# Layer norm's scaling on VectorE, with mean and power as its two scalars

## The chip, the cores and the metric

The kernel runs on one core of a Trainium2 chip. The metric is the device time of one execution in microseconds (us), as the median of several runs. Beside it stands one execution that the hardware profiler recorded.

## What is computed

All of it is float32, for 8 batches of 576 tokens and 512 channels. Three blocks follow one another: an attention without a score matrix, a gated MLP with a mixing over tokens, and a spatial product of rank 32 with a channel MLP. The change lies in the second block:

```python
h = x @ w_in
h = 0.5 * h * (1.0 + np.tanh(c * (h + 0.044715 * h ** 3)))
u, v = (h[..., :d_ff // 2], h[..., d_ff // 2:])
mu = np.mean(v, axis=-1, keepdims=True)
var = np.mean((v - mu) ** 2, axis=-1, keepdims=True)
v_n = (v - mu) / np.sqrt(var + 1e-06) * g_ln
v_s = np.einsum('ts,bsd->btd', w_sg, v_n) + b_sg[None, :, None]
gated = u * v_s
x = x + gated @ w_out
```

The layer norm goes over the 512 columns of v, for each token.

## The kernel before, in words

There are two stages. In the first, until about 600 us, the kernel goes through the batches 0 to 7; in the second it does the large channel products for all tokens, in five groups. Beside the first stage the weights of the channel products are converted and written back to memory (tiles stg, f, chw), a piece at a time, on ScalarE, GpSimd and VectorE. Every product is made of float32 pieces: an operand is split into a high part (a ScalarE copy) and a low part (a subtraction, `low`, on VectorE or GpSimd), and three products are summed.

A batch b goes as follows. x comes as xh and xl. Then, for the five tiles t of 128 tokens (the fifth has 64), `emit_Vh` multiplies x by half of w_in into a PSUM tile pv, and ScalarE's gelu writes it to the SBUF tile ge (three buffers; L616, L620). `stats` takes mean and variance into the two columns of mv (L626 to L628), on VectorE: bn_stats, bn_aggr and the addition of epsilon; GpSimd then raises the second column to the power -0.5 (L629). `emit_ln` (L632) scales: VectorE makes shift = -mean * power (the tile sh, L636), ScalarE does ge = ge * power + shift (L639), ScalarE copies ge to the high part vh, and the low part vl is subtracted by GpSimd, for the fifth tile by VectorE, into the upper half of vh. All five vh and vl stay until the mixing over tokens, `emit_S` (PSUM tile pS, L671).

The loop at L1284 calls `emit_ln` for tile t - 1 behind `stats` of tile t, and for the fifth tile behind the first product of `emit_Uh` (PSUM tiles pu, L657; there are four, and gelu takes them to ut). Between the tiles stand other pieces of work: the transposed y of the batch before (yh, yl), its rank-32 product (pp, pst) and the addition of its result to y (`emit_PV`, PSUM tile pw, VectorE's addition yt, L762), and for the next batch the maxima of q (qm) and of k (km; `k_max` transposes the folded maximum, PSUM tile pm, L423). pv, pw, pu, pS and py share three PSUM buffers ("big"). After `emit_Uh` come the exponentials of the next batch's q and k, `emit_S`, and `emit_y` with the product by w_out (py), whose operands gh and gl are the split gated tile gt.

What sets the order: TensorE's and, in the batch loop, VectorE's instructions run in the order in which the program names them (`manual_schedule`, `in_order(dve)`). The queues of ScalarE, GpSimd and SP, which issues the DMAs, are ordered in the batch loop when the program is built, by a simulated timeline. In the second stage all are in program order.

In batch 7 the buffers of ge are reused for the tiles us, with which the second stage's operands uh and ul are made (`u_parts`, L794; the load is L800).

Of the kernel before, what the change touches and what calls it, by code (L numbers as in the profile page):

```python
# [8 lines left out]
F32 = mybir.dt.float32  # L9
F32R = mybir.dt.float32r  # L10
U32 = mybir.dt.uint32
AF = mybir.ActivationFunctionType
ALU = mybir.AluOpType
# [9 lines left out]
def fused_kernel(tc, q, k, v, w_in, g_ln, w_sgT, b_sg, w_out, U, V, w_ch1, w_ch2, outT):  # L23
    nc = tc.nc
    B, S, C = q.shape
    P = 128
# [22 lines left out]
    pe, act, dve, pool, sp = nc.tensor, nc.scalar, nc.vector, nc.gpsimd, nc.sync  # L49
# [10 lines left out]
    def copy(out, src):  # L60
        return act.activation(out, src, AF.Copy)  # L61

    def low(eng, out, src, hi):
        return tt(eng, out, src, as_f32(hi), ALU.subtract)

    def opened(name, bufs=1, **kw):
        cm = tc.tile_pool(name=name, bufs=bufs, reuse_waits="tile", **kw)
        return cm.__enter__(), lambda: cm.__exit__(None, None, None)
# [17 lines left out]
    tmpp, close_tmpp = opened("tmpp", 2, side="left")  # L86
# [545 lines left out]
    def emit_ln(b, t):  # L632
        ge, mv = ln.pop((b, t))
        n = TR[t]
        shift = tmpp.tile([P, 1], F32, tag="sh", name="sh", bufs=4)
        dve.scalar_tensor_tensor(  # L636
            out=shift[0:n], in0=mv[0:n, 0:1], scalar=-1.0, in1=mv[0:n, 1:2], op0=ALU.mult, op1=ALU.mult
        )
        act.activation(ge[0:n], ge[0:n], AF.Identity, bias=shift[0:n], scale=mv[0:n, 1:2])  # L639
        h = wrk.tile([P, F], F32R, tag=f"vh{t}", name=f"vh{t}")  # L640
        if t < NT:
            l = wrk.tile([P, F], F32R, tag=f"vl{t}", name=f"vl{t}")
            copy(h, ge)
            low(pool, l, ge, h)
            vh[b, t] = (h, l)
        else:
            copy(h[0:R], ge[0:R])
            low(dve, h[64 : 64 + R], ge[0:R], h[0:R])
            vh[b, t] = h
# [620 lines left out]
    for b in range(B):  # L1270
# [13 lines left out]
        for t in range(NT + 1):  # L1284
            emit_Vh(b, t)
            if nxt:
                with behind(dve):
                    for t2 in Q_MAX[b > 0][t]:
                        q_max(nxt, t2)
                    for _ in range(FOLDS[b > 0][t]):  # L1290
                        next(fold)
            if t < NT:
                stats(b, t)
            slot(TURNS[b][0][t])
            if t > 0:
                emit_ln(b, t - 1)
            if t == NT:
                stats(b, t)
            if b > 0:
                for t2 in ((2,), (3, 4), (), (), ())[t]:  # L1300
                    emit_yT(b - 1, t2)
            if t == 2 and b > 0:
                for t2 in range(NT + 1):
                    emit_U(b - 1, t2)
            if b > 0:
                for c in ((), (), (), (0, 1), (2, 3))[t]:
                    emit_PV(b - 1, c)
# [16 lines left out]
        for f in range(NF):  # L1324
            if nxt and f == spread_at:
                k_spread(nxt)
            if b == 0:
                slot(TURNS[b][1][f])
            if not nxt:
                for _ in range((0, 2, 2, 2)[f]):  # L1330
                    next(prep, None)
            emit_Uh(b, f)
            if f == 0:
                emit_ln(b, NT)
                if nxt:
                    load_v(nxt)
                else:
                    next(prep, None)
            if nxt:
                for t in Q_SUB[b > 0][f]:  # L1340
                    q_sub(nxt, t, pool if t in Q_SUB_POOL[b > 0] else dve)
                for t in K_SUB[b > 0][f]:
                    if f >= spread_at:
                        k_sub(nxt, t)
                    else:
                        late_k.append(t)
                if f == spread_at:
                    for t in late_k:
                        k_sub(nxt, t)
            if b > 0:  # L1350
                slot(TURNS[b][1][f])
# [181 lines left out]
```

## Time and profile before

| | us |
|---|---|
| median of 3 runs | 1314.13 |
| lowest and highest run | 1310.84 and 1314.26 |
| the profiled execution | 1313.29 |
| its span, from the first to the last instruction | 1311.5 |

| engine | busy us | share of the span | instructions |
|---|---|---|---|
| TensorE (PE) | 1261.5 | 96% | 7576 |
| VectorE (DVE) | 982.4 | 75% | 1426 |
| ScalarE (ACT) | 654.9 | 50% | 997 |
| GpSimd (POOL) | 346.2 | 26% | 440 |

The mean granted TensorE clock is 0.993 of full speed. Busy times are sums over the whole span; the two stages differ, so what an engine is worth is to be read from the stretch in which it works. A line of a timeline gives start and duration in us, engine, line of the kernel, operation, output and inputs, shape and count, and in brackets how long the engine stood idle before it and what ended that. Instructions of one line merge into a row with a count.

### The profile page before, as it was taken

The page shows a single profiled execution, that of the slowest core. Times are in us where ns is not written, and L with a number is a line of the kernel's source. Part 1 is how long each engine was busy: PE and PEld are TensorE (multiplying, and loading weights), DVE is VectorE, ACT ScalarE, POOL GpSimd, SP SyncE. Part 2 cuts the span into 40 slices and gives each one's busy share as a digit, 9 for nine tenths or more (in the row PEclk, how much of TensorE's full clock was granted, in tenths as well). Part 3 has the DMA queues.
Part 4 walks back from the last instruction along what each step waited for, and adds up shares of the span by engine and source line. Part 5 has one row for each costly group of instructions (what it writes and reads, how often), then busy time and mean ns, then how long its engine had stood idle before and what let it go on. Part 6 is the DMA issues. An engine that isn't in the chain of part 4 may idle for free.

```text
span 1311.5 us, 20618 instructions
## 1 busy us (share of the span) xinstructions
PE 1261.5 (96%) x7576; PEld 1137.7 (87%) x7576; DVE 982.4 (75%) x1426; ACT 654.9 (50%) x997; POOL 346.2 (26%) x440
## 2 busy tenths in 40 slices
PE   4799999999999999998999999999999999999998
PEld 2598998989898989888788888888888889999998
DVE  8898979798897979779668953598337963694485
ACT  3756757565766666655454522444134422451342
POOL 3743253633434253666340202000010002000000
PEclk9999999999999999998999999999999999999999
DMA  7525162533425261468998677678766788898886
GB/s 249 166 62 171 37 189 66 171 124 120 142 100 170 76 189 67 156 226 280 322 357 306 227 239 258 209 240 289 258 194 225 245 286 296 275 307 303 261 291 213
DMA packets 135908, 274.15 MB, mean 209 GB/s; under 512 B 15232, under 2 KB 56704, under 8 KB 135808
## 3 DMA queue, kind: packets, MB, share of 16 engines
q1 hardware_dynamic: 135808, 272.84, 63.0%
q8 instruction: 60, 0.98, 0.3%
q14 instruction: 40, 0.33, 0.1%
HBM read 224.56 MB, written 48.23 MB: 208 GB/s over the span
## 4 chain that ended last, share of the span: by engine, by line
PE 72%; DVE 14%; DMA 5%; ACT 3%; POOL 3%; issue 3%; SPq 0%; DVEq 0%; POOLq 0%; ACTq 0%
PE mm L52 50%; PE pv L52 5%; PE pS L52 4%; PE pu L52 4%; PE py L52 3%; DMA stg<-in_w_ch_dram 2%; PE pm L52 1%; DMA qt<-in_q_dram 1%; DVE qt L55 1%; DVE f L187 1%; PE pp L52 1%; POOL chw L55 1%; DVE gt L681 1%; DVE bst L626 1%; PE pt L714 1%
## 5 line engine op out<-in xcount | busy, mean ns | idle before, releaser
L52 PE MATMUL mm<-oh,wu 128*128 128x512 f32 (+1 forms) x1120 | 320.5, 367 | 0.0
L52 PE MATMUL mm<-uh,wu 128*128 128x512 f32 (+1 forms) x1064 | 303.6, 366 | 1.7 <-DVE h L55 0.8
L52 PEld LDWEIGHTS mm<-oh,wu 128*128 128x128 f32 x1120 | 207.1, 188 | 26.3
L52 PEld LDWEIGHTS mm<-uh,wu 128*128 128x128 f32 x1064 | 196.4, 188 | 26.8 <-DVE h L55 1.0
L52 PE MATMUL mm<-ol,wu 128*128 128x512 f32 (+1 forms) x560 | 205.5, 367 | 0.0
L61 ACT ACTIVATE oh<-h 128x1024 fp32r<-128x1024 f32 (+1 forms) x140 | 135.2, 973 | 124.8 <-PE mm L52 102.4
L52 PE MATMUL mm<-ul,wu 128*128 128x512 f32 (+1 forms) x532 | 194.7, 366 | 0.0
L55 DVE TENSOR_TENSOR ol<-h,oh 128x1024 fp32r<-128x1024 f32 (+1 forms) x140 | 155.4, 1113 | 41.0 <-ACT oh L61 40.1
L55 POOL TENSOR_TENSOR ust<-ust 128x1024 f32<-128x1024 f32 (+1 forms) x16 | 36.3, 2276 | 389.8 <-DMA ust<-u2d 349.8
L55 DVE TENSOR_TENSOR h<-mm,u 128x1024 f32<-128x1024 f32 (+1 forms) x57 | 63.3, 1111 | 88.1 <-PE mm L52 88.1
L52 PEld LDWEIGHTS mm<-ol,wu 128*128 128x128 f32 x560 | 105.1, 188 | 13.0
L55 DVE TENSOR_TENSOR u<-mm,u 128x1024 f32<-128x1024 f32 (+1 forms) x53 | 58.9, 1111 | 76.7 <-PE mm L52 72.0
L52 PEld LDWEIGHTS mm<-ul,wu 128*128 128x128 f32 x532 | 99.9, 188 | 12.0
L55 POOL TENSOR_TENSOR chw<-f,chw 128x256 fp32r<-128x256 f32 x98 | 78.4, 816 | 89.6 <-ACT chw L61 84.6
L55 DVE TENSOR_TENSOR h<-h,h 128x1024 f32<-128x1024 f32 (+1 forms) x80 | 88.9, 1112 | 0.0
L1057 ACT ACTIVATE h<-mm 128x1024 f32<-128x1024 f32 (+1 forms) x19 | 17.8, 937 | 131.8 <-PE mm L52 131.8
L1048 ACT ACTIVATE h<-h 128x1024 f32<-128x1024 f32 (+1 forms) x60 | 58.1, 968 | 33.6 <-DVE h L55 33.6
L61 ACT ACTIVATE u<-mm 128x1024 f32<-128x1024 f32 (+1 forms) x24 | 22.5, 938 | 103.4 <-PE mm L52 87.2
L61 ACT ACTIVATE chw<-f 128x256 fp32r<-128x256 f32 x112 | 42.7, 411 | 59.5 <-DVE f L188 22.1
L175 POOL TENSOR_SCALAR stg<-stg 128x256 f32<-128x256 f32 (+1 forms) x83 | 43.4, 527 | 89.8 <-DMA stg<-in_w_ch_dram 48.1
L52 PE MATMUL py<-gh,wo_h 128*128 128x288 f32 x256 | 57.8, 308 | 3.6 <-DVE gt L681 2.4
L52 PE MATMUL py<-gl,wo_h 128*128 128x288 f32 x256 | 56.6, 304 | 4.2 <-DVE gl L55 4.2
(174 smaller groups left out, 2695.2 us busy)
## 6 DMA issues: line engine op xcount, KB each, us to landing
wu<-wd SPq DMA_DIRECT2D x280, 512.0 KB, 4.4
wd<-chw SPq DMA_DIRECT2D x112, 256.0 KB, 3.5
stg<-in_w_ch_dram SPq DMA_DIRECT2D x64, 256.0 KB, 3.8
u2d<-yt SPq DMA_DIRECT2D x32, 288.0 KB, 2.3
vt<-in_v_dram SPq DMA_DIRECT2D x32, 256.0 KB, 6.7
qt<-in_q_dram SPq DMA_DIRECT2D x7, 1024.0 KB, 7.0
kt<-in_k_dram SPq DMA_DIRECT2D x7, 1024.0 KB, 7.0
res<-u2d SPq DMA_DIRECT2D x12, 512.0 KB, 5.0
```

The source lines that it names most:

```text
L52: pe.matmul(out, lhsT, rhs, start=first, stop=last, skip_group_check=onto)
L55: return eng.tensor_tensor(out=out, in0=a, in1=b, op=op)
L61: return act.activation(out, src, AF.Copy)
L175: eng.tensor_scalar(out=hi, in0=hi, scalar1=F64_MOST, scalar2=-F64_MOST, op0=ALU.min, op1=ALU.max)
L187: dve.tensor_scalar(out=b, in0=b, scalar1=3, scalar2=None, op0=ALU.logical_shift_left)
L626: dve.bn_stats(out=bst[0:n], in_=ge[0:n])
L681: dve.scalar_tensor_tensor(out=two(gt), in0=halves(pS), scalar=gl[:, f : f + 1], in1=two(bb), op0=ALU.mult, op1=ALU.add)
L714: pe.transpose(pt[0:n, c * P : (c + 1) * P], y_t[b][:, c, t * P : t * P + n], ident)
L1048: act.activation(h, h, AF.Relu)
L1057: act.activation(h_out(j, 11, n), bank, AF.Relu)
```

## The change

`emit_ln` loses the tile sh, its VectorE product and ScalarE's scaling. One VectorE instruction takes their place; it subtracts the mean and multiplies by the power, with both columns of mv as scalars, and writes ge in place. The copy to vh and the low part stay as they were.

```diff
@@ -632,11 +632,9 @@
     def emit_ln(b, t):
         ge, mv = ln.pop((b, t))
         n = TR[t]
-        shift = tmpp.tile([P, 1], F32, tag="sh", name="sh", bufs=4)
-        dve.scalar_tensor_tensor(
-            out=shift[0:n], in0=mv[0:n, 0:1], scalar=-1.0, in1=mv[0:n, 1:2], op0=ALU.mult, op1=ALU.mult
+        dve.tensor_scalar(
+            out=ge[0:n], in0=ge[0:n], scalar1=mv[0:n, 0:1], scalar2=mv[0:n, 1:2], op0=ALU.subtract, op1=ALU.mult
         )
-        act.activation(ge[0:n], ge[0:n], AF.Identity, bias=shift[0:n], scale=mv[0:n, 1:2])
         h = wrk.tile([P, F], F32R, tag=f"vh{t}", name=f"vh{t}")
         if t < NT:
             l = wrk.tile([P, F], F32R, tag=f"vl{t}", name=f"vl{t}")
```

## Rows read from the trace of the kernel before

**Rows 1.** The page: span, and busy time of the engines.

```profile
span 1311.5 us, 20618 instructions
...
PE 1261.5 (96%) x7576; PEld 1137.7 (87%) x7576; DVE 982.4 (75%) x1426; ACT 654.9 (50%) x997; POOL 346.2 (26%) x440
```

**Rows 2.** Stretches: length, then busy time and count by engine, PEclk, DMA.

```profile
45.00:110.00 65.00, 54.43 (x405) 51.31 (x405) 59.70 (x116) 39.18 (x76) 35.24 (x37) 0.92 0.29 85
75.00:100.00 25.00, 22.26 (x227) 21.52 (x225) 24.52 (x43) 13.81 (x26) 9.83 (x9) 1.00 0.20 61
175.00:240.00 65.00, 63.63 (x468) 59.20 (x468) 52.70 (x96) 42.14 (x68) 27.31 (x38) 1.00 0.41 125
573.00:595.00 22.00, 17.79 (x130) 17.33 (x129) 21.69 (x31) 11.96 (x25) 12.55 (x14) 0.95 0.58 196
```

**Rows 3.** Timeline of TensorE's weight loads, batch 0: rows with a wait.

```profile
62.25 0.72 PEld L423 LDWEIGHTS pm<-ident,km 128*128 128x128 f32 x4 [7.38 <-DVE km L55]
...
100.04 0.30 PEld L52 LDWEIGHTS py<-gh,wo_h 128*128 128x128 f32 x2 [2.65 <-ACT qh L61]
```

**Rows 4.** The same in batch 2, up to the next one with a wait.

```profile
208.44 0.30 PEld L52 LDWEIGHTS pw<-v_w,pst 128*128 128x128 f32 x2 [0.31 <-DVE yt L55]
209.11 0.30 PEld L52 LDWEIGHTS pw<-v_w,pst 128*128 128x128 f32 x2 [0.37 <-DVE yt L55]
210.03 0.30 PEld L52 LDWEIGHTS pu<-xh,wih 128*128 128x128 f32 x2 [0.18 <-DVE ge L55]
238.40 2.41 PEld L52 LDWEIGHTS pk<-vt,kt 128*64 128x64 f32 x80 [0.16 <-issue]
```

**Rows 5.** Timeline of VectorE in batch 2, third and fourth tile.

```profile
207.45 0.15 DVE L636 SCALAR_TENSOR_TENSOR sh<-mv 128x1 f32<-128x1 f32 x1
207.63 1.42 DVE L55 TENSOR_TENSOR yt<-pw,yt 128x576 f32<-128x576 f32 x2
209.29 0.68 DVE L55 TENSOR_TENSOR ge<-pv,ge 64x512 f32<-64x512 f32 x1 [0.23 <-ACT ge L61]
209.90 1.25 DVE L636 SCALAR_TENSOR_TENSOR sh<-mv 128x1 f32<-128x1 f32 x1
```

**Rows 6.** Timeline of GpSimd in batch 2, the same time.

```profile
205.52 1.72 POOL L55 TENSOR_TENSOR vl<-ge,vh 128x512 fp32r<-128x512 f32 x1 [1.10 <-ACT vh L61]
...
209.86 1.28 POOL L55 TENSOR_TENSOR vl<-ge,vh 128x512 fp32r<-128x512 f32 x1 [1.63 <-ACT vh L61]
```

**Rows 7.** Groups by line, ScalarE: busy us, mean ns, idle before, releaser.

```profile
L639 ACT ACTIVATE ge<-ge,sh,mv 128x512 f32<-128x512 f32 (+1 forms) x40 | 32.6, 814 | 40.7 <-DVE sh L636 40.6
```

**Rows 8.** The same groups, VectorE.

```profile
L636 DVE SCALAR_TENSOR_TENSOR sh<-mv 128x1 f32<-128x1 f32 (+1 forms) x40 | 23.4, 586 | 0.0
...
L628 DVE TENSOR_SCALAR mv<-mv 128x1 f32<-128x1 f32 (+1 forms) x40 | 6.1, 152 | 1.4
...
L55 DVE TENSOR_TENSOR vh<-ge,vh 64x512 fp32r<-64x512 f32 x8 | 5.5, 685 | 12.6 <-ACT vh L61 12.6
```

**Rows 9.** Timeline of VectorE in batch 0: a clamp.

```profile
91.95 0.28 DVE L175 TENSOR_SCALAR stg<-stg 128x256 f32<-128x256 f32 x1
```

**Rows 10.** The chain of waits, in order of time, batch 2.

```profile
210.08 6.60 PE pu L52 x48
```

**Rows 11.** Timeline of VectorE, fifth tile in batch 0, then in batch 7.

```profile
71.65 1.62 DVE L636 SCALAR_TENSOR_TENSOR sh<-mv 64x1 f32<-64x1 f32 x1
...
563.75 2.72 DVE L636 SCALAR_TENSOR_TENSOR sh<-mv 64x1 f32<-64x1 f32 x1
568.02 0.69 DVE L55 TENSOR_TENSOR vh<-ge,vh 64x512 fp32r<-64x512 f32 x1 [1.55 <-ACT vh L61]
...
572.53 0.95 DVE L55 TENSOR_TENSOR ul<-us,uh 128x512 fp32r<-128x512 f32 x1 [2.77 <-ACT uh L61]
```

**Rows 12.** Timeline of SP's DMA queue in batch 7: the load of us.

```profile
568.73 0.32 SPq L800 DMA_DIRECT2D us<-u2d  x1
```

**Rows 13.** Timeline of TensorE's weight loads in batch 7.

```profile
594.63 0.50 PEld L52 LDWEIGHTS py<-gl,wo_h 128*128 128x128 f32 x2 [3.16 <-DVE gl L55]
```

## The prediction

> **What bounds the kernel now.** I read the page's busy line first. TensorE is busy 1261.5 of 1311.5 us [rows 1]; a change on other engines can win back at most the 50 us in between, and only where TensorE waits for what is changed. The table of stretches says where those 50 us lie: in the stretch of batch 0 that holds its layer norm TensorE lacks 65 - 54.43 = 10.6 us, in 65 us of an inner batch 1.4 us, in 22 us of batch 7 4.2 us [rows 2]. VectorE is busy 59.70, 52.70 and 21.69 us there, so it is the next engine after TensorE; ScalarE has 39.18, 42.14 and 11.96 and is nobody's bound. The change moves work from the engine with room to the one without.
>
> Then I went through TensorE's weight-load queue for its waits. In batch 0 it waits 7.38 us for the last fold of k's maximum and 2.65 us at the first product with w_out [rows 3]. The second is put down to a ScalarE copy, but VectorE comes in at 24.52 busy of 25 us before it [rows 2], so VectorE paces it. In batch 2 the waits near the layer norm are 0.31, 0.37 and 0.18 us, and from 210 to 238 us there is none [rows 4]: the two products pw wait for VectorE's additions yt, the first product pu for VectorE's addition ge. Most inner batches repeat this within a few tenths. In batch 7 TensorE waits 3.16 us for gl [rows 13].
>
> **The change, part by part.** It removes 40 ScalarE instructions of 0.814 us, 32.6 us in all, in front of which ScalarE idled 40.7 us for sh [rows 7]. ScalarE doesn't bound, so the 32.6 us by themselves are worth nothing; what counts is that the scaled tile is ready sooner.
>
> It removes 40 sh of 23.4 us on VectorE [rows 8]. Their work is short: sh without a hindrance takes 0.15 us [rows 5], 6.0 us for 40. The other 17.4 us are waits inside the instruction. Batch 2 shows for what: sh at 209.90 ends at 211.15, as GpSimd's vl does (209.86 + 1.28) [rows 5, 6].
>
> It adds 40 tensor_scalar over 512 columns, of which this trace has none. Lower end: the clamp, the same instruction with two constants, takes 0.28 us for 256 columns [rows 9], and one column takes 0.152 us [rows 8]; half a nanosecond a column gives 0.152 + 511 x 0.0005 = 0.41 us. Upper end: the pace of the low part vh over 512 columns, 0.685 us [rows 8]. I take 0.41, since the clamp is the same operation on the same kind of data and only its scalars differ. VectorE then gains 0.41 - 0.15 = 0.26 us of work for each of 40, 10.4 us; at the upper end 0.54 us, 21.4 us. The waits for GpSimd I leave at 17.4 us: GpSimd still makes the power and vl.
>
> The chain from the power to the copy vh gets shorter: 0.26 us more on VectorE, 0.814 less on ScalarE, so 0.55 us sooner at the lower end and 0.28 at the upper. ScalarE issues nothing else for it, no DMA is removed or added, and SP's queue is passed by nothing.
>
> Where does that reach TensorE?
>
> Inner batches, third layer-norm tile: sh at 207.45 stands ahead of two yt, and VectorE goes from sh to yt without idling [rows 5]. The new instruction makes yt 0.26 us later, and the two pw with it. But VectorE idles 0.23 us before the addition ge [rows 5], which releases the first pu; so pu comes only 0.03 us later. Six batches: 0.2 us. At the upper end it is 0.54 - 0.23 = 0.31 us, 1.9 us for six.
>
> Fourth tile: the 1.25 us of sh at 209.90 are a wait for vl of the tile before [rows 5, 6]. This vl starts 0.55 us sooner, as its copy does, and ends near 210.6; the new instruction waits about 0.5 us less. That puts the last tile's vl ahead of the small addition of epsilon, which may wait in its stead. I count this stall as moved, at nothing; what covers it is 3.3 us of the first pu (half of the 6.60 us that the chain gives two) [rows 10] before the next pu wants the bank of the next yt.
>
> Fifth tile: VectorE idles 12.6 us over eight batches before the low part vh, which waits for the copy, which waits for the scaling [rows 8]. It shrinks by about 0.55 us per batch. In an inner batch that pays for two of the five 0.26 us, and with the shorter wait at the fourth tile the rest; TensorE goes through pu and pS until past 238 us without a wait [rows 4], so nothing comes of it: 0.
>
> Batch 0: VectorE works through from that vh to the place of the 2.65 us wait [rows 2, 3], so 0.55 us sooner there is 0.55 us off the wait. Before the 7.38 us wait lie two of the new instructions and a clamp that waits for vl; I set these against each other: 0, with +0.5 and -0.5 as ends.
>
> Batch 7: the vh at 568.02 releases a buffer of ge, which the load issued at 568.73 waits for; its data come before the copy uh that VectorE's ul at 572.53 waits for, after 2.77 us of idleness [rows 11, 12]. From there VectorE is busy 21.69 of 22 us [rows 2] up to the 3.16 us wait [rows 13]. So 0.55 us here, too.
>
> **Sum:** +0.2 - 0.55 - 0.55 = -0.9 us. The profiled execution took 1313.29 us (span 1311.5 and 1.8 around it), so 1312.4; the runs' median of 1314.13 lies 0.8 above that execution, so I put 1313.2 on record. What a measurement of this kernel can tell from no change is about 0.3%, 3.9 us: that is no change.
>
> **Rivals.** *VectorE sets the pace: slower.* The place is the third tile in the inner batches. GpSimd's vl of the second tile ended at 207.24 there, 0.2 us before sh [rows 5, 6]. If ScalarE's or GpSimd's order shifts so that a vl (1.28 us) lies in the way, yt is late by 0.26 plus up to 1.28 us; all beyond the 0.23 us of idleness goes to TensorE one for one: 1.3 us in each of seven batches, 9.2 us on top of the forecast, 1322.4. For it: VectorE is the fullest engine after TensorE. Against: the copy and with it vl move away from that place, not toward it. The Trainium skill (Perfetto Trace Analysis, Optimizing Scalar/DVE Operations) advises to move work from VectorE to ScalarE where VectorE is full, the reverse of this change; no run shown here tests that. Its page SBUF — State Buffer (Who interferes with whom) adds that such an instruction holds a port pair against GpSimd for its whole length, while ScalarE never waits for anyone; the ends of sh and vl above agree for the waiting side. One chance in five.
>
> *The waits for GpSimd go with sh: faster.* The fifth sh took 2.72 us in batch 7 and 1.62 us in batch 0 [rows 11]; both lie on the stretches that VectorE paces. If the new instruction came ahead of GpSimd's work at both, 2.6 and 1.5 us more would go: 1313.2 - 4.1 = 1309.1. Against: GpSimd is still given vl and the power first. One in six.
>
> *The order of other queues.* TensorE and VectorE are ordered by hand here, but ScalarE, GpSimd and SP by a simulated timeline, which sees 40 instructions less. ScalarE could load its tables in another order or a copy could stand behind a later wait. What a batch shows of such sizes is 0.5 to 3 us [rows 3, 13], of either sign. It widens the range on both sides and has one in eight.
>
> *It does not do what it says*, with the instruction at the pace of vh: the upper ends above, +1.9 - 0.28 - 0.28 = +1.3 us instead of -0.9, so 1315.4, still no change. It is inside the forecast's case.
>
> **Numbers.** No change, near 1313.2: 0.51. VectorE's pace: 0.20. Waits gone: 0.16. Another order: 0.13, split about 0.05 faster, 0.04 same, 0.04 slower. The faster rival falls short of the bound about one time in eight (0.02 to the same). That gives faster 0.19, same 0.57, slower 0.24. The range takes in both rivals' times, and leaves out about one case in eight beyond them: 1308.5 to 1322.5.
>
> **What would show it.** Right: the new instruction near 0.41 us where GpSimd is idle; ScalarE 32 us less busy; VectorE within 10 us of before; the idle time before vh near 1 us per batch; the waits of 2.65 and 3.16 us half a microsecond shorter; 0.31 and 0.37 us at pw a little longer and pu as before. Wrong: a new wait of a microsecond at pw or pu in every batch, new waits at pv, or other table loads on ScalarE.

## The result and the profile after

The changed kernel takes 1323.86 us (median of 4 runs, 1321.64 to 1324.75), the kernel before in the same comparison 1312.99 (1310.84 to 1314.26). The ratio is 1.0084, with an interval from 1.0071 to 1.0096: **slower by 0.84%**, 11 us, where no change was forecast and the range ended at 1322.5.

First the page of the changed kernel, the lines that answer to [rows 1]:

```profile
span 1321.9 us, 20559 instructions
...
PE 1260.1 (95%) x7576; PEld 1136.2 (86%) x7576; DVE 996.3 (75%) x1426; ACT 610.5 (46%) x947; POOL 354.6 (27%) x440
```

TensorE does the same work in a span that is 10.4 us longer, so it waits more. ScalarE lost 44.4 us: the 40 scalings (32.6) and 10 table loads of 1.283 us went, and its other instructions took 1.0 us more. VectorE gained 13.9 us, where the forecast's own value was 10.4.

The groups of VectorE by line (busy us, mean ns | idle before) say where the 13.9 us are. They answer to [rows 8]:

```profile
L635 DVE TENSOR_SCALAR ge<-ge,mv 128x512 f32<-128x512 f32 (+1 forms) x40 | 28.7, 718 | 0.5 <-POOL mv L55 0.5
...
L55 DVE TENSOR_TENSOR km<-km,kt 128x512 f32<-128x512 f32 x24 | 26.1, 1087 | 1.5 <-DMA kt<-in_k_dram 0.8
L55 DVE TENSOR_TENSOR vh<-ge,vh 64x512 fp32r<-64x512 f32 x8 | 5.9, 732 | 5.6 <-ACT vh L61 5.6
```

The new instruction has 28.7 us where sh had 23.4: +5.3. The larger term is an instruction that the change doesn't touch: km, the fold of k's maximum. In the kernel before its group read

```profile
L55 DVE TENSOR_TENSOR km<-km,kt 128x512 f32<-128x512 f32 x24 | 17.8, 742 | 1.6 <-DMA kt<-in_k_dram 0.9
```

so the folds cost 8.3 us more. What they wait for shows in batch 2, where VectorE's and GpSimd's rows are laid side by side. The kernel before, second and third tile: folds on VectorE, vl on GpSimd (start us, us):

```profile
202.06 0.69 DVE L55 TENSOR_TENSOR km<-km,kt 128x512 f32<-128x512 f32 x1
...
203.69 0.24 DVE L636 SCALAR_TENSOR_TENSOR sh<-mv 128x1 f32<-128x1 f32 x1
...
204.68 1.42 DVE L55 TENSOR_TENSOR km<-km,kt 128x512 f32<-128x512 f32 x2
```

```profile
202.07 1.84 POOL L55 TENSOR_TENSOR vl<-ge,vh 128x512 fp32r<-128x512 f32 x1 [2.10 <-ACT vh L61]
```

And the changed kernel, the same place:

```profile
206.00 1.67 DVE L55 TENSOR_TENSOR km<-km,kt 128x512 f32<-128x512 f32 x1
...
208.59 0.54 DVE L635 TENSOR_SCALAR ge<-ge,mv 128x512 f32<-128x512 f32 x1
209.16 0.70 DVE L55 TENSOR_TENSOR pst<-pp,pst 32x512 fp32r<-32x512 f32 x1
209.89 2.39 DVE L55 TENSOR_TENSOR km<-km,kt 128x512 f32<-128x512 f32 x2
...
213.21 0.54 DVE L635 TENSOR_SCALAR ge<-ge,mv 128x512 f32<-128x512 f32 x1
213.77 1.42 DVE L55 TENSOR_TENSOR yt<-pw,yt 128x576 f32<-128x576 f32 x2
```

```profile
205.62 1.49 POOL L55 TENSOR_TENSOR vl<-ge,vh 128x512 fp32r<-128x512 f32 x1 [1.88 <-ACT vh L61]
208.75 0.78 POOL L55 TENSOR_TENSOR mv<-mv,half 128x1 f32<-128x1 f32 x1 [1.64 <-DVE mv L628]
209.93 1.80 POOL L55 TENSOR_TENSOR vl<-ge,vh 128x512 fp32r<-128x512 f32 x1 [0.39 <-ACT vh L61]
```

Whoever is there first goes, and the other waits inside its instruction. Before, a fold was first (202.06 against 202.07; the pair at 204.68 against vl at 205.52 [rows 6]): the folds took 0.69 to 0.71 us, and vl 1.84 and 1.72 instead of 1.28. Afterwards vl is first at 205.62 and ends at 207.11; the fold of 206.00 ends 0.56 us behind it. The other vl, at 209.93, comes 0.04 us after the first fold of a pair began, is served between the two, ends at 211.73, and the second fold ends 0.55 us behind that. Before, vl came 1.59 us after sh had ended (205.52 - 203.93), now 0.80 us after the new instruction has ended (209.93 - 209.13): the 0.8 us are ScalarE's scaling, which stood between them. Counted from the start of sh and of the new instruction, vl comes 0.49 us sooner (1.83 us behind it before, 1.34 now), and the pair of folds 0.31 us later (0.99 and 1.30), because the new instruction is longer than sh. Both bring vl nearer to the pair's start: before, it came 0.84 us behind it, now 0.04. The Trainium skill (SBUF — State Buffer, Who interferes with whom) describes the port pair that VectorE and GpSimd share as an exclusive lock; these rows agree, in both directions.

The third view is TensorE's weight loads with a wait, batch 2, to be read against [rows 4]:

```profile
209.91 0.57 PEld L52 LDWEIGHTS pw<-v_w,pst 128*128 128x128 f32 x4 [1.07 <-DVE pst L55]
214.59 0.30 PEld L52 LDWEIGHTS pw<-v_w,pst 128*128 128x128 f32 x2 [2.45 <-DVE yt L55]
215.25 0.30 PEld L52 LDWEIGHTS pw<-v_w,pst 128*128 128x128 f32 x2 [0.37 <-DVE yt L55]
```

0.31 us at pw became 1.07 + 2.45. From the first fold to yt VectorE takes 213.77 - 205.29 = 8.48 us; before, 207.63 - 201.36 = 6.27 (the first fold of a batch starts at 205.29 and 201.36). Of the 2.2 us the folds are 2.0, the two layer-norm instructions 0.7, and 0.3 us of VectorE's idle time before the statistics went.

Over the whole kernel (TensorE's waits by releaser: us, times, longest), before and after:

```profile
PEld pw L52 <- DVE yt L55: 5.5, 14, 1.0
...
PEld pw L52 <- DVE pst L55: 1.3, 2, 0.9
```

```profile
PEld pw L52 <- DVE yt L55: 15.9, 14, 2.5
...
PEld pw L52 <- DVE pst L55: 3.7, 4, 1.1
```

Last, the loss by batch. The time from one batch's first load of pk to the next one's is taken as a beat (238.40 us in batch 2 [rows 4]); batch 1's begins at batch 0's pk, and batch 7's ends at the first mm. Beside it stands how many of the batch's folds took 1.65 us or more, which the rows of tile km in each batch's stretch give; these are batches 2 and 3 of the changed kernel (count, then min/median/max in ns, first and last start):

```profile
L55 DVE TENSOR_TENSOR km<-km,kt x3: 692/1666/1670, 206.0 to 210.6; 128x512 f32<-128x512 f32 x3
```

```profile
L55 DVE TENSOR_TENSOR km<-km,kt x3: 691/692/1648, 277.2 to 280.8; 128x512 f32<-128x512 f32 x3
```

| beat, us | batch 1 | 2 | 3 | 4 | 5 | 6 | 7 |
|---|---|---|---|---|---|---|---|
| before | 74.8 | 70.3 | 69.8 | 69.0 | 69.3 | 69.6 | 117.8 |
| after | 78.1 | 73.2 | 70.2 | 70.1 | 70.1 | 72.7 | 117.5 |
| difference | +3.2 | +2.9 | +0.4 | +1.0 | +0.8 | +3.2 | -0.3 |
| folds that waited, before | 0 | 0 | 1 | 0 | 0 | 0 | no folds |
| folds that waited, after | 2 | 2 | 1 | 1 | 1 | 2 | no folds |

All of the loss is in batches 1 to 6, and it goes with the folds. Batch 7 has five of the new instructions and no folds, and loses nothing. In batch 3 a fold waited before, too, so the change adds none there: that is the batch with the smallest loss.

The two places of the folds are not worth the same. In batches 3, 4 and 5 it is the second fold of the pair that waits, and TensorE waits for yt alone, 1.49 us in each (before 0.30 us in batch 4); this is batch 4:

```profile
354.82 0.30 PEld L52 LDWEIGHTS pw<-v_w,pst 128*128 128x128 f32 x2 [1.49 <-DVE yt L55]
```

In batches 1, 2 and 6 the single fold ahead of pst waits as well. There pw waits first for pst (1.09, 1.07 and 0.86 us) and then 2.45 us for yt: both waits are about 1 us longer than in batches 3 to 5. Why the second grows with the first isn't shown.

### The profile page after: what moved, and what is told of

Same layout as the page of the kernel before. It is cut to its first block, busy times and chain, and to the rows that moved or that the text cites. A ratio compares the mean times of both kernels' runs of the same rounds, so it can differ in the third digit from the quotient of the medians.

```text
span 1321.9 us, 20559 instructions
## 1 busy us (share of the span) xinstructions
PE 1260.1 (95%) x7576; PEld 1136.2 (86%) x7576; DVE 996.3 (75%) x1426; ACT 610.5 (46%) x947; POOL 354.6 (27%) x440
## 4 chain that ended last, share of the span: by engine, by line
PE 70%; DVE 17%; DMA 5%; issue 2%; POOL 2%; ACT 2%; SPq 0%; DVEq 0%; POOLq 0%; ACTq 0%
PE mm L52 50%; PE pS L52 6%; PE pu L52 6%; PE py L52 4%; DVE km L55 2%; DMA stg<-in_w_ch_dram 2%; DVE bst L626 1%; PE pv L52 1%; DVE f L187 1%; DMA wd<-chw 1%; DVE f L188 1%; PE pm L52 1%; DVE qm L465 1%; DVE yt L55 1%; POOL chw L55 1%
## 5 line engine op out<-in xcount | busy, mean ns | idle before, releaser
L61 ACT ACTIVATE chw<-f 128x256 fp32r<-128x256 f32 x112 | 42.8, 412 | 69.2 <-DVE f L188 24.6
L1046 ACT ACTIVATE h<-h 128x1024 f32<-128x1024 f32 (+1 forms) x60 | 58.1, 969 | 33.8 <-DVE h L55 33.8
```

Source lines behind the costliest of these rows:

```text
L1046: act.activation(h, h, AF.Relu)
```

## The experiments

**Theory A**: the folds, which now wait for vl, make the loss. **Theory B**: VectorE's list paces this stage, and the length of the new instruction ahead of yt makes it.

**A ScalarE copy put back in front of vh**, to make vl late again:

```diff
+        copy(ge[0:n], ge[0:n])
         h = wrk.tile([P, F], F32R, tag=f"vh{t}", name=f"vh{t}")
```

> The changed kernel with one more ScalarE copy of ge onto itself between the new instruction and the copy vh, about 0.6 us: vl comes back to nearly its old place, the new instruction stays. Theory A (collision: GpSimd's vl, which now comes sooner, is ahead of VectorE's folds km, whose two inputs wait for it): km's mean falls from 1.09 us back under 0.85, the wait at pw from 1.5 to 2.5 us back under 1 us, and the time to 1315 to 1319; what remains is the new instruction's own length. Theory B (length: the new instruction takes 0.54 us for sh's 0.15, three times ahead of yt in each batch): the time stays at 1321 to 1326, as ScalarE's copy changes nothing on VectorE.

1324.84 us, ratio 1.0104 [1.0084, 1.0124]. km stayed at 1.107 us in the mean: the copy delayed vl by less than the scaling had (vl 1.40 us behind the end of the new instruction at the place named here, against 1.59 behind sh and 0.80 without the copy), and vl still met a fold (vl at 423.66, the pair of folds at 423.01 took 2.47 us). What was to be brought about didn't come about, so this run decides nothing.

**The change for some tiles only**: the third to fifth (e2), the first two (e3), the fifth alone (e7); the others keep sh and the scaling.

```diff
+        if t >= 2:
             dve.tensor_scalar(...)
+        else:
+            (sh and act.activation as before)
```

> The new instruction for the third to fifth tile of a batch alone, the first two as before. The vl of the first two tiles are those that stand beside the folds km. Theory A (collision): km is back at 0.74 us, and the time within 3 us of before, 1311 to 1316. Theory B (length): one of the three longer instructions ahead of yt is left, a third of the loss, 1315 to 1318, with km as it may be.

> The reverse: the new instruction for the first two tiles alone. Theory A (collision): km stays at 1.0 us or over and nearly the whole loss is there, 1320 to 1325. Theory B (length): two thirds of it, 1318 to 1321, and km is no guide.

> The new instruction for the fifth tile alone. VectorE's idle time before the fifth tile's low part shrinks from 12.6 to under 7 us, and no vl of the first tiles moves. Theory A: 1309 to 1314, so the 1.1 us that the prediction put on batches 0 and 7 are there or are lost in the spread. Theory B: 0 to a fifth of the loss, 1311 to 1315. What it asks is whether a part of the change is worth having; it hardly tells the theories apart.

e2: 1315.32 us, 1.0027 [1.0014, 1.0039], km 0.691; its batches 1 to 6 are no longer than before (the pk of batch 6 stands at 515.3, before at 516.1), and what its profiled execution loses comes in batch 7 (119.4 against 117.8 us). e7: 1312.83, 1.0015 [1.0002, 1.0028], km 0.695. e3: 1332.91, 1.0158 [1.0127, 1.0189], km 1.201: the two tiles whose vl stand near the folds lose by themselves more than the whole change does, 12.5 us of it in batches 1 to 6, in each of which two folds wait; and the sh of the later tiles wait for GpSimd again (0.819 us in the mean). So the loss is made by the first two tiles, which A and B both allow (both have the instruction ahead of yt there); km goes with it each time.

**The same instruction with constants 0 and 1** (the tile is not scaled, and nothing waits for the power):

```diff
-            ..., scalar1=mv[0:n, 0:1], scalar2=mv[0:n, 1:2], ...
+            ..., scalar1=0.0, scalar2=1.0, ...
```

> The changed kernel with the constants 0 and 1 as the two scalars in place of the two columns of mv, so the tile isn't scaled and the instruction doesn't wait for the power. It asks what the length of 0.54 us is made of: by the clamp of the kernel before it should take 0.41 us, and the two columns as scalars then cost 0.13. Theory A: the time hardly moves, 1321 to 1325, since vl still comes soon. Theory B: three times 0.13 us less ahead of yt in seven batches, 1320 to 1322.

1323.12 us, 1.0089 [1.0068, 1.0111]. The tile rows of ge give the length, of the changed kernel and of this one:

```profile
L635 DVE TENSOR_SCALAR ge<-ge,mv x40: 527/538/2342, 56.1 to 574.1; 128x512 f32<-128x512 f32 x32, 64x512 f32<-64x512 f32 x8
```

```profile
L635 DVE TENSOR_SCALAR ge<-ge x40: 408/419/1285, 56.4 to 572.1; 128x512 f32<-128x512 f32 x32, 64x512 f32<-64x512 f32 x8
```

A median of 0.419 against 0.538 us: two columns as scalars cost 0.12 us over two constants. The loss stayed although the instruction was 0.12 us shorter; km was 1.024. Once more km and the time stayed together, without a proof of which makes which.

**The folds as an instruction with one input**, four reductions over 128 columns x 5 in batches 1 to 7, in the changed kernel (e5) and in the one before (e6):

```diff
-        tt(dve, m, kt[:, 0], kt[:, 1], ALU.max)
...
+            yield dve.tensor_reduce(
+                out=m[:, cs], in_=kt[:, :, cs].rearrange("p t c -> p c t"), op=ALU.max, axis=mybir.AxisListType.X
+            )
```

> The changed kernel, with the maximum of k over the five tiles (batches 1 to 7) taken by four tensor_reduce over a quarter of the columns each, in place of four tensor_tensor. They have one input from SBUF where km's had two; qm, of the same kind, took 0.68 us whatever GpSimd did. Theory A (collision of km with vl): nothing waits for vl any more at that place, the wait at pw falls under 1 us and the time to 1312 to 1318, though four reductions may be 0.1 us longer each. Theory B (length of the new instruction): the reductions are no shorter, so 1321 to 1326.

> The control: the same reductions in the kernel before. Both theories: within 4 us of before, 1309 to 1316, since km met vl only once in a while there.

1329.32 us, 1.0130 [1.0113, 1.0147], and 1321.60, 1.0074 [1.0059, 1.0089]. The reduction was too dear for the test:

```profile
L421 DVE TENSOR_REDUCE km<-kt 128x128 f32<-128x640 f32 x28 | 35.4, 1302 | 0.2
```

1.30 us each, where the expectation had put 0.1 us more than a fold. VectorE's busy time grew by 13.8 us in the kernel before (982.4 to 996.2) and by 6.4 us in the changed one (996.3 to 1002.7), whose folds had waited 8.3 us until then. The control lost 9.9 us by that alone, and so showed that VectorE's list does reach TensorE when it grows by as much as 2 us a batch at this place. A's forecast for the changed kernel, 1312 to 1318 us, did not come in. And the pair says something for B: no reduction waits for vl (the longest takes 1.34 us), yet the change still costs 7.7 us between the two kernels (e6, then e5):

```profile
PEld pw L52 <- DVE yt L55: 12.2, 14, 1.5
```

```profile
PEld pw L52 <- DVE yt L55: 19.4, 14, 2.6
```

The longest wait in a batch goes from 1.5 to 2.6 us, and the three new instructions ahead of yt are 3 x 0.39 = 1.2 us longer than three sh, which fits: in this longer list their length is no longer covered. Behind three of e5's six waits of 2.6 us (batches 1, 2 and 4) TensorE ran for 3.4 us with a granted clock of 0.50, its lower level of 1.2 GHz; e6 has no such stretch in batches 1 to 6. By an estimate from these stretches, half of 3 x 3.4 us, some 5 us of the difference come in that way.

**Length without the change**: a multiplication by 1 plus 0 ahead of sh in the kernel before, for all five tiles (e8), then for the first three (e10), since e8 put new waits for GpSimd at the last two.

```diff
+        if t < 3:
+            dve.tensor_scalar(out=ge[0:n], in0=ge[0:n], scalar1=1.0, scalar2=0.0, op0=ALU.mult, op1=ALU.add)
         shift = tmpp.tile([P, 1], F32, tag="sh", name="sh", bufs=4)
```

> The kernel before with a tensor_scalar on ge (times 1, plus 0, by constants, so nothing is computed by it; 0.41 us) ahead of each sh: VectorE has 0.41 + 0.15 = 0.56 us per tile as with the new instruction, but ScalarE's scaling still stands between it and vl, so vl keeps its place behind sh. Theory A: without the earlier vl there is no collision; 1313 to 1318, and km under 0.85 us. Theory B: the same length at the same place costs the same, 1320 to 1326.

> The kernel before, with one added VectorE instruction (times 1 plus 0, both constants, 0.41 us by the run with constants) ahead of sh for the first three tiles alone, so that nothing is put ahead of the fourth and fifth tile, where such an instruction waited for GpSimd in an earlier run. It lengthens VectorE's list by 24 x 0.41 = 9.8 us and starts no vl sooner. Theory B (length ahead of yt goes to TensorE nearly one to one): 1318 to 1322 us. Theory A (length is hidden, only the folds' waits for vl count): 1312 to 1314 us, km 0.70 to 0.78.

e8: 1325.26 us, 1.0106 [1.0091, 1.0121], km 0.815. e10: 1322.49 us, 1.0074 [1.0059, 1.0089], km 0.814. By the time alone both speak for B. By batch e8 still does: its list has 33.8 us of added instructions, waits for GpSimd included, and 10.1 us less in sh, 3 us a batch, and batches 1 to 6 are together 7.7 us longer (430.6 against 422.9), batches 4 and 5 by 1.5 and 1.2 us without a fold that waits. By batch e10 does not: its beats are 74.4, 69.2, 70.4, 69.2, 69.1, 70.6 and 123.8 us. Batches 1 to 6, with three added instructions in each and a fold that waits in three of them, are together 0.1 us shorter than before; 1.4 us are lost by the pk of batch 0, 6.0 in batch 7 and 1.8 behind it, most of batch 7's at one place, a wait of TensorE that neither the kernel before nor the changed one has:

```profile
641.21 0.30 PEld L52 LDWEIGHTS mm<-uh,wu 128*128 128x128 f32 x2 [3.95 <-DVE yt L55]
```

Behind this wait TensorE ran at its lower level (granted clock 0.50 from 643 to 646 us). So 1.2 us a batch ahead of yt are covered in the inner batches, where the change makes its loss, and e8's 3 us only in part. Why batch 7 answers so strongly here, and not to the change, stays open.

**vl taken out of the folds' way**: in batches 1 to 6 ScalarE writes vl of the first two tiles as zeros, so the rounding remainder of V is left out there. VectorE's list stays as it is. With it the same in the kernel before.

```diff
-            low(pool, l, ge, h)
+            if 0 < b < B - 1 and t < 2:
+                act.activation(l, ge, AF.Identity, scale=0.0)
+            else:
+                low(pool, l, ge, h)
```

> The changed kernel, with the low parts vl of the first two tiles of batches 1 to 6 written by ScalarE (zeros: the rounding remainder of V is left out there) instead of GpSimd's two-input subtraction. VectorE's list is unchanged, and no vl of GpSimd can meet a fold any more. The folds km took 1.087 us in the mean after the change and 0.742 before it, 8.3 us over 24. Theory A (most of the loss is the folds' waiting for vl): km falls to about 0.70 us and the time to 1315 to 1318 us. Theory B (only the instruction's length on the path to yt counts, the folds' waits are taken up elsewhere): km falls too, but the time stays at 1321 to 1325 us. The added ScalarE work, 12 times some 0.8 us, is put at 0 to 1 us, since ScalarE got rid of 32.6 us and 40 added copies cost 1.0 us in an earlier run.

> The control: the same replacement of the two vl in the kernel before. Its folds took 0.742 us in the mean against 0.69 undisturbed, so 1.2 us over 24 folds is all that could be won on them, and ScalarE, which here still does the scaling, gets 12 more instructions. Theories A and B: both 1310 to 1314 us, km about 0.69. A time well above that would say that the added ScalarE work itself costs time, and the run on the changed kernel would have to be read against this one.

1311.51 us, ratio 0.9999 [0.9987, 1.0010] for the changed kernel, and 1311.33, 0.9994 [0.9985, 1.0003] for the one before. **The whole loss is gone**, and the control gains nothing. The groups of the first, and TensorE's waits at pw:

```profile
L635 DVE TENSOR_SCALAR ge<-ge,mv 128x512 f32<-128x512 f32 (+1 forms) x40 | 28.6, 714 | 0.7 <-POOL mv L55 0.7
...
L55 DVE TENSOR_TENSOR km<-km,kt 128x512 f32<-128x512 f32 x24 | 17.2, 717 | 1.5 <-DMA kt<-in_k_dram 0.8
```

```profile
PEld pw L52 <- DVE yt L55: 8.2, 14, 1.4
```

The new instruction costs VectorE 28.6 us (28.7 in the changed kernel), and that costs the kernel nothing; of VectorE's groups only the folds went back by more than 1.2 us, by 8.9 us, and pw's wait with them. For the kernel as it is this decides for A; in the longer list of e5 the length did cost time. A had expected 6 to 9 us of it to go; all of it went.

**The layer norm of the third and fourth tile behind yt**, in the changed kernel:

```diff
-            if t > 0:
+            if t > 0 and not (b > 0 and t >= 3):
                 emit_ln(b, t - 1)
...
                     emit_PV(b - 1, c)
+            if b > 0 and t >= 3:
+                emit_ln(b, t - 1)
```

> The changed kernel, with the layer norm of the third and fourth tile emitted behind the additions to yt that it stood ahead of (batches 1 to 7): 0.54 us less of VectorE's list stands ahead of yt at each of 14 places, 7.6 us in all; the folds and the vl that they wait for stay as they are (km 1.0 to 1.1 us). Theory B (length): 1315 to 1318 us. Theory A (the folds' waits): 1321 to 1325 us. Both together (about 60 per cent waits, 40 per cent length): 1317 to 1321 us, unless the fourth tile's later vh and vl hold up something behind them.

1326.80 us, 1.0109 [1.0092, 1.0126], km 1.106. The time came out above A's range, too. TensorE's wait at pw for yt did fall, from 15.9 to 12.5 us, but vl came later and GpSimd's diag behind it, and pb now waited 7.0 us for diag in 12 places, which it did in none before. With a gain and a new loss in one run it doesn't tell the theories apart.

**The folds moved**, with all the work kept: two of them a tile earlier (e12, and e14 in the kernel before), all four two places and one place earlier than their last (e13, ahead of the second tile's statistics; e15, and e16 in the kernel before, ahead of the third's).

```diff
-    FOLDS = ((0, 1, 2, 1, 0), (0, 0, 2, 2, 0))
+    FOLDS = ((0, 1, 2, 1, 0), (0, 2, 2, 0, 0))
```

> The changed kernel, with the table of the folds turned from (0, 0, 2, 2, 0) to (0, 2, 2, 0, 0) for batches 1 to 6: the first two folds stand one tile earlier, ahead of the second tile's statistics, and the other two ahead of the third tile's; none stands ahead of the fourth tile's, where vl of the second tile met one. The instruction, its length and all of GpSimd's work stay, and nothing is left out. Theory A (the loss is the folds' waiting for vl): only the third tile's folds can meet a vl, one a batch, so km falls to 0.75 to 0.95 us and the time to 1313 to 1319 us. Theory B (length of the instruction): the time stays at 1321 to 1325 us. If the k block has not landed when the earlier folds want it, VectorE waits for it there and the time stays high with km low and a wait for that DMA in its place.

> The control, and a candidate: the kernel before with the folds at (0, 2, 2, 0, 0). It had one fold of 1.82 us in seven batches, so the folds can give back about 1 us; whether their earlier place costs anything by itself shows here. Theories A and B: 1310 to 1315 us, km 0.69 to 0.75 us.

> The changed kernel with all four folds of batches 1 to 6 ahead of the second tile's statistics, (0, 4, 0, 0, 0): every fold is done before the first vl of its batch can start. Theory A: km about 0.70 us and 1311 to 1315 us, as in the run in which ScalarE wrote the two vl, plus at most 1 to 2 us for waiting for the k block and for the second tile's later statistics. Theory B: 1321 to 1325 us.

> The changed kernel with all four folds of batches 1 to 6 ahead of the third tile's statistics, (0, 0, 4, 0, 0). The k block has landed by then, so no fold waits for it (as in the run with all four ahead of the second tile's), and only the vl of the first tile can meet a fold, one a batch. If the loss goes by the folds' waits for vl: km 0.75 to 0.90 us and 1312 to 1317 us, unless the third tile's later statistics or pst (which comes after them) hold up TensorE in their place, which would show as a longer wait of pw for pst. If the fold's place hardly counts: 1319 to 1324 us.

> The kernel before with the same place of the folds, the control and a candidate. Its vl of the first tile came in the middle of the two folds that stand there and waited for them; with four folds in a row the same should hold, so km 0.69 to 0.80 us, and the time 1310 to 1316 us. A time of 1319 to 1324 us with km over 0.90 would repeat what the place (0, 2, 2, 0, 0) did to this kernel: a fold that waits for vl costs the kernel before as much as the changed one.

| folds of batches 1 to 6 | before: us, km | changed: us, km |
|---|---|---|
| (0, 0, 2, 2, 0), as given | 1312.99, 0.742 | 1323.86, 1.087 |
| (0, 2, 2, 0, 0), e14 and e12 | 1322.52, 0.941 | 1316.31, 0.938 |
| (0, 0, 4, 0, 0), e16 and e15 | 1319.45, 0.944 | 1322.56, 0.987 |
| (0, 4, 0, 0, 0), e13 | not run | 1319.88, 0.717 |

Against the kernel before as given the ratios are e12 1.0033 [1.0021, 1.0045], e14 1.0071 [1.0054, 1.0087], e13 1.0064 [1.0049, 1.0079], e15 1.0072 [1.0049, 1.0095], e16 1.0053 [1.0034, 1.0071]. Of A's forecasts e12 came in (1313 to 1319 us), e13 (1311 to 1315) and e15 (1312 to 1317) did not. Two controls missed theirs, and that teaches most: the kernel before loses 7 to 10 us from nothing but the place of its folds, and at (0, 2, 2, 0, 0) the change *saves* 6.2 us. In batch 1 of e14 a fold waits 1 us for a vl, in the same batch of e12 hardly (longest fold 0.84 us); so it is in batch 2, while in batches 3 to 6 one fold waits in both:

```profile
L55 DVE TENSOR_TENSOR km<-km,kt x3: 673/693/1677, 128.7 to 133.1; 128x512 f32<-128x512 f32 x3
```

```profile
L55 DVE TENSOR_TENSOR km<-km,kt x3: 691/692/843, 127.9 to 132.8; 128x512 f32<-128x512 f32 x3
```

The mean of km doesn't tell the whole time, though: e12 and e14 have nearly the same. At this place the folds stand ahead of pst, the operand of pw, and what they wait goes to pw at another row (e12, then e14):

```profile
PEld pw L52 <- DVE pst L55: 11.6, 7, 2.1
...
PEld pw L52 <- DVE yt L55: 5.4, 14, 1.4
```

```profile
PEld pw L52 <- DVE pst L55: 11.7, 7, 2.1
PEld pw L52 <- DVE yt L55: 9.6, 14, 1.0
```

In e15, with all four folds ahead of pst, pw waits 14.7 us for it. e13 has no fold in batches 1 to 6 that waits for vl and still loses: four folds stand ahead of yl, in batches 3, 5 and 6 the first of them waits 1.2, 2.0 and 0.5 us for the k block to land, and yl makes TensorE wait at pp:

```profile
PEld pp L52 <- DVE yl L55: 9.1, 6, 2.7
```

Most of its loss is in batches 3 and 5, whose beats are 3.8 and 4.6 us longer than before. Behind the waits of 2.44 and 2.73 us at pp there TensorE ran for 3.4 us at its lower level, half of its clock, which costs some 1.7 us each time (an estimate: half of 3.4). In batch 3 (stretch and busy times as in [rows 2], granted clock third from the end):

```profile
275.00:278.00 3.00, 3.00 (x8) 2.33 (x8) 1.97 (x5) 0.98 (x2) 1.64 (x2) 0.50 0.00 0
```

No place that was tried keeps the change without its loss, and no version here beats the kernel before.

## Why the prediction was wrong

- **The step that failed** is the one that follows the earlier vl. The prediction had it ("this vl starts 0.55 us sooner") and looked for what it meets at the fourth tile alone; of the third tile it said, against its own slower rival, that "the copy and with it vl move away from that place, not toward it", and it put the third tile at 0.03 us a batch. Vl did move, 0.49 us forward from the start of VectorE's instruction, close to the forecast, and 0.80 us against the folds, which the longer instruction pushes back. That brought it into the folds, which stand between the layer norm and yt and were not in the argument. One or two folds a batch waited about 1 us each, 8.3 us in all, TensorE's waits at pw for yt and pst went from 6.8 to 19.6 us, and the kernel lost 11 us.
- **The rival** "VectorE sets the pace" had the place (yt, pw, the inner batches, a vl of 1.28 us in the way), the size (9.2 us forecast, some 11 measured) and the view that would show it (a wait of a microsecond at pw in every batch). Its mechanism was half right: vl holds up VectorE, but not at the new instruction, and it comes from the change itself and not from a shift of other queues. The chance of one in five was too low because the argument against it rested on the direction in which vl moves, and no row had been read for what stands on VectorE at its new time.
- **The size of the new instruction** was 0.41 us by the clamp with constants, and 0.538 measured. For constants the estimate was right (0.419); what its working left out is what two columns as scalars cost. Inside the bounds (0.41 to 0.685), and worth nothing by itself in this kernel: e9 has the full length and no loss. It had a share in the collision, though: 0.31 of the 0.80 us.
- **Length hidden**: right for the inner batches (e9, and e10 by its beats). It held for a reason that the prediction had too narrowly, 0.23 us of idle time before ge; e10 shows 1.2 us a batch covered. It has an end: 2 to 3 us a batch are covered only in part (e6, e8), and on top of e6's list the change's own length costs time (e5).
- **The waits inside sh** were left at 17.4 us; the new instruction has 28.7 - 40 x 0.538 = 7.2 us of them. The fifth one in batch 0 fell from 1.62 [rows 11] to 0.53 us, and the wait for the copy before vh from 12.6 to 5.6 us over eight batches, as forecast (by 7.0; 0.55 x 8 = 4.4 had been expected).
- **Batch 0**: the first py, at 100.04 [rows 3], came 2.0 us sooner instead of 0.55,

```profile
98.02 0.30 PEld L52 LDWEIGHTS py<-gh,wo_h 128*128 128x128 f32 x2 [1.42 <-ACT qh L61]
...
107.48 0.30 PEld L52 LDWEIGHTS py<-gh,wo_h 128*128 128x128 f32 x2 [1.91 <-ACT wo_h L61]
```

  though the wait for wo_h at 107.48 is 0.9 us longer (1.91 against 1.01 us at 109.52). Part of it is the clock, which the prediction did not have: in the kernel before, TensorE ran behind its 2.65 us wait from 101 to 105 us mostly at its lower level (granted clock 0.50 from 101.5 to 104.5 us), in the changed kernel at 1.00. The 2.0 us are still there at the first pv of batch 1 (118.62 against 120.67) and gone at the pw that waits for yt, which comes 1.8 us later (139.90 against 138.10): pv waits 0.81 and 0.31 us, pw 1.09 and 2.45. Behind that last wait the changed kernel has such a stretch, too (0.50 from 142 to 144.5 us). The 7.38 us [rows 3] became 7.46: nothing, as put.
- **Batch 7**: 0.55 us were forecast; the 3.16 us wait [rows 13] stayed at 3.16. TensorE came to it 1.7 us sooner (76.8 against 78.5 us behind the pk of batch 6), but then waited 1.85 us at pp for yh instead of 0.47, and the batch was 0.3 us shorter.
- **ScalarE** was to lose 32 us and lost 44.4, ten table loads among them: the rival of other queue orders came about, at no cost that e9 shows.

What stays open: why a fold that waits ahead of pst shows in two waits of TensorE, so that two waiting folds cost a batch 3 us and one more than before only 0.8 to 1.0; and where between e10's 1.2 and e6's 2 us a batch the room ends. That the loss is the folds' waiting is shown for the vl of the first two tiles together (e9), not for each.

## What to carry to other kernels

When a change makes a result ready sooner, find out what its consumer will then run beside: here the gain on a free engine started GpSimd's subtraction 0.5 us sooner, the longer instruction started the folds 0.3 us later, and a fold on VectorE that had nearly always gone first went second. Read both engines' rows at the new time, and price each instruction of two inputs that stands between there and the next thing TensorE wants. And look at the loss by batch before believing a total: e10's total spoke for one theory and its batches for the other. Length that costs nothing in one order can cost in another: that it is covered holds for the list in which it was measured.

## What was not expected of the hardware

- A tensor_scalar over 512 columns takes 0.538 us with two columns as scalars, 0.419 us with two constants.
- A reduction over five planes, 128 columns out of 640, takes 1.30 us on VectorE, about 2 ns for each column read; a two-input maximum over 512 columns takes 0.69 us.
- VectorE's maximum of two inputs and GpSimd's subtraction of two inputs never overlap in full in the rows shown: the second takes 1.67 us instead of 0.69, or 1.84 instead of 1.28.
- GpSimd's power of one column takes 0.56 us in the median where it starts outside the new instruction and 0.72 to 0.79 us in the 18 of 40 places where it starts inside it (0.78 at 208.75): the new instruction holds up GpSimd as well.
